# One transfer for the gate weights, and the first loads moved ahead of the opening barrier, in a fused attention and adapter kernel

## The chip, the cores and the metric

The kernel runs on one core of a Trainium2 chip. The metric is the device time of one execution in microseconds (us). The kernel before took 256.07 us (median of 3 runs, 255.68 to 256.32). Runs come with a state: "fast" unless they lie over 1.5% above the fastest of their kernel, "unknown" for a single run. The core has five instruction streams: TensorE (PE), VectorE (DVE), ScalarE (ACT), GpSimd (POOL) and SyncE (SP). Three of them issue transfers here: SyncE, ScalarE and GpSimd. The transfers are done by 16 DMA engines. Each load reports that it has landed by 16 increments of a semaphore. Below, a "ring" is the share of a load behind one of these increments, and a load has landed when the last of its 16 rings has.

## The reference, cut to what matters

```python
# q, k, v: 4 x 6400 x 256 float32
qn = q / (np.linalg.norm(q, axis=1, keepdims=True) + 1e-06)
kn = k / (np.linalg.norm(k, axis=1, keepdims=True) + 1e-06)
a  = softmax(kn.transpose(0, 2, 1) @ qn / tau)      # 256 x 256 per batch
x  = (v @ a).reshape(25600, 256)
logits = x @ w_gate                                  # 256 x 8; the two largest of 8 experts are kept
# delta = sum over the two experts of  weight * (x @ A[e]) @ B[e],   A[e]: 256 x 16, B[e]: 16 x 256
return x + delta
```

Only one thing of it matters: q and k of the first batch must be on the core before any matmul can run, and the gate weights, A and B (`moe_w_gate`, `moe_A`, `moe_B`) are small and needed much later, at about 35 us.

## The kernel before: the parts that matter

The first two columns of chunks of q and k come in as float32 by SyncE and ScalarE, whose transfers do not cast. ScalarE casts them. All else of q, k and v comes in through GpSimd, whose transfers cast to bf16 under way. The first such GpSimd load is the rest of the first piece of q (called "GpSimd's q" below), the second the same part of k ("GpSimd's k").

```python
    def load_consts():
        first = W["first"].rearrange("p c d -> p (c d)")
        W["A0"] = first[0:P // 4, 4 * C:8 * C].rearrange("p (e g r) -> p e g r", e=E, r=R)
        nc.sync.dma_start(W["A0"], moe_A.rearrange("e (p g) r -> p e g r", g=8))
        W["B0"] = first[:, 8 * C:9 * C]
        nc.scalar.dma_start(W["B0"], moe_B.rearrange("e r d -> (e r) d"))
        W["wg0"] = first[:, 9 * C:9 * C + CC * E].rearrange("p (cc e) -> p cc e", e=E)
        wg = moe_w_gate.rearrange("(p g cc) e -> g p cc e", g=4, cc=CC)
        for g in range(4):
            nc.scalar.dma_start(W["wg0"][g * (P // 4):(g + 1) * (P // 4)], wg[g])

    def do_load(s, what, b, i, c, n):
        # ... cut: choice of the tile t and the source src
            if (b, c) == (0, 0):
                # ... cut
                (nc.sync if what == "q" else nc.scalar).dma_start(W[what], src[b, :, 0:n, :])
                return
        nc.gpsimd.dma_start(t[:, c - c0:c - c0 + n, :], src[b, :, c:c + n, :])

    # ... cut; the steps are emitted in a planned order:
    for s in steps:
        do[s.key[0]](s, *s.key[1:])
        if s.key[0] == "load":
            n_load += 1
            if n_load == 2:
                load_consts()
            if n_load == 4:
                make_consts()
```

The program that is built from this has two blocks at its start. The first, called "main" below, is not in the kernel's text: GpSimd writes four constants (memsets), then every engine has a DRAIN instruction, then comes an opening barrier. The second block, the "body", holds the kernel.

## Time and profile before

| | before |
|---|---|
| time | 256.07 us |
| span in the profile | 254.4 us |
| PE busy | 85% |
| DMA engines | 90% busy or more in all but the first and last of 40 slices |
| first byte moves | 1.75 us |
| GpSimd's q issued, landed | 1.24 us, 10.22 us |
| GpSimd's k issued, landed | 1.90 us, 14.72 us |
| last matmul ends | 246.3 us |

First the strip of 40 equal slices and the DMA queues, from the page of the kernel before. A digit is a busy share in tenths, 9 being 90% or more. The queues show packets, megabytes and the share of the 16 engines' span that the packets took. q0 is GpSimd's, and here carries its casting loads. q1 and q10 carry what SyncE and ScalarE issue.

```profile
DMA  8999999999999999999999999999999999999994
...
q0 software_dynamic: 7488, 39.06, 74.7%
q1 hardware_dynamic: 3968, 26.61, 25.7%
q10 hardware_dynamic: 480, 0.40, 0.7%
```

Next, the timeline of the start of the kernel before: start, duration, engine, line, operation, and in brackets how long the engine was idle before and what released it ("issue": nothing that the profile shows).

```profile
0.34 0.10 POOL L926 MEMSET const-uint8-127<- 128x1 uint8 x1
0.74 0.40 ACTq L541 DMA_DIRECT2D y<-in_k_dram  x1
0.74 0.38 SPq L541 DMA_DIRECT2D y<-in_q_dram  x1
...
1.24 0.66 POOL L543 DMA_DIRECT2D qk<-in_q_dram  x1 [0.79 <-POOLq L926]
1.66 2.02 ACTq L483 DMA_DIRECT2D y<-in_moe_w_gate_dram  x4
1.90 0.54 POOL L543 DMA_DIRECT2D qk<-in_k_dram  x1
...
3.70 1.28 ACT L497 ACT_TABLE_LOAD   x1 [3.70 <-issue]
...
14.76 1.84 PEld L558 LDWEIGHTS <-qk 128*128 128x128 bf16 x10 [7.92 <-DMA qk<-in_k_dram]
```

SyncE and ScalarE issue their first loads at 0.74 us, right behind the barrier, and GpSimd at 1.24 us. ScalarE then spends 2.02 us on four gate transfers. From 14.76 us on PE works on what GpSimd's k brought. These waits are what the change aims at.

### The profile page before, as it was taken

To read this page: it belongs to the slowest core of one execution; us is meant where nothing else is said; L and a number is where in the kernel's file an instruction comes from. 1 tells how busy PE (TensorE), PEld (TensorE's weight loads), DVE (VectorE), ACT (ScalarE), POOL (GpSimd) and SP (SyncE) were. 2 spreads that over 40 slices of the span, in tenths; PEclk is the share of its full clock that TensorE was granted. 3 is DMA by queue.
4 is the path that set the end of the run, shared out by engine and by line. 5 is a ranking of instruction groups with operands and counts; after the bars stand their busy time and mean duration, and the time that the engine had idled before them with its cause. 6 is when DMAs were issued, how large, how long until landed. Compare 5 with 4: busy or idle time off the path is not lost.

```text
span 254.4 us, 6345 instructions
## 1 busy us (share of the span) xinstructions
PE 217.1 (85%) x2641; PEld 193.2 (76%) x2643; DVE 189.6 (75%) x483; ACT 166.7 (66%) x270; POOL 30.0 (12%) x58
## 2 busy tenths in 40 slices
PE   0165984899999998999989999889999979999970
PEld 0053962598999996799789998779999759999860
DVE  0055589779889977898979995689888878888910
ACT  3344446558786766888768667543777859768770
POOL 7000220040020002000130100510000200000000
PEclk9999997599999999999999999999999999999995
DMA  8999999999999999999999999999999999999994
GB/s 188 215 218 208 211 220 213 213 220 215 213 218 210 317 293 293 259 216 219 210 215 220 214 216 216 214 208 353 276 287 320 337 315 315 321 426 422 423 411 174
DMA packets 11964, 66.47 MB, mean 261 GB/s; under 512 B 1568, under 2 KB 2464, under 8 KB 7328
## 3 DMA queue, kind: packets, MB, share of 16 engines
q0 software_dynamic: 7488, 39.06, 74.7%
q1 hardware_dynamic: 3968, 26.61, 25.7%
q10 hardware_dynamic: 480, 0.40, 0.7%
q8 instruction: 20, 0.33, 0.5%
q14 instruction: 8, 0.07, 0.1%
HBM read 78.91 MB, written 26.21 MB: 413 GB/s over the span
## 4 chain that ended last, share of the span: by engine, by line
PE 54%; DMA 34%; DVE 3%; ACT 3%; POOL 2%; issue 1%; DVEq 0%; ACTq 0%; POOLq 0%
DMA qk<-in_k_dram 28%; PE Y_ps L877 13%; PE Y_ps L881 7%; PE T_ps L753 7%; DMA v<-in_v_dram 6%; PE ZL_ps L775 5%; PE gzT_ps L864 3%; PE acc_417 L558 2%; PE acc_418 L558 2%; PE acc_2620 L558 2%; PE acc_2621 L558 2%; PE Z_ps L844 2%; DVE a_bf L727 2%; POOL qk L543 1%; PE log_ps L790 1%
## 5 line engine op out<-in xcount | busy, mean ns | idle before, releaser
L586 DVE TENSOR_TENSOR ssq<-ssq,sq 128x1280 f32<-128x1280 f32 (+1 forms) x27 | 43.4, 1607 | 26.7 <-ACT sq L580 24.7
L877 PE MATMUL Y_ps<-a_bf,vT 128*128 128x256 bf16 x400 | 60.0, 273 | 0.0
L580 ACT ACTIVATE sq<-qk 128x1280 f32<-128x1280 bf16 (+1 forms) x27 | 36.8, 1364 | 25.9 <-DVE ssq L586 19.3
L733 ACT COPY y<-Y_ps 128x512 f32<-128x512 f32 x79 | 45.8, 587 | 12.2 <-PE Y_ps L881 9.6
L558 PEld LDWEIGHTS <-qk 128*128 128x128 bf16 x400 | 33.8, 103 | 24.9 <-DMA qk<-in_k_dram 15.3
L733 ACT COPY vT<-T_ps 128x1024 bf16<-128x1024 bf16 (+1 forms) x44 | 37.0, 871 | 7.7 <-PE T_ps L753 7.5
L877 PEld LDWEIGHTS <-vT 128*128 128x128 bf16 x400 | 37.6, 98 | 3.7
L881 PE MATMUL Y_ps<-ball,gzT 128*128 128x256 bf16 x200 | 38.2, 273 | 0.3 <-DVE gzT L735 0.3
L558 PE MATMUL acc_110<-qk 128*128 128x256 bf16 x50 | 15.0, 310 | 16.9 <-DMA qk<-in_k_dram 10.6
L753 PE MATMUL T_ps<-ident,v 128*128 128x128 bf16 x400 | 28.0, 224 | 0.6 <-DMA v<-in_v_dram 0.6
L543 POOL DMA_DIRECT2D v<-in_v_dram x20 | 12.2, 612 | 128.7 <-PE T_ps L753 81.5
L562 PEld LDWEIGHTS <-qk 128*128 128x128 bf16 x242 | 24.3, 100 | 3.4
L753 PEld LDWEIGHTS <-v 128*128 128x128 bf16 x400 | 24.6, 100 | 1.9 <-DMA v<-in_v_dram 1.5
L881 PEld LDWEIGHTS <-gzT 128*128 128x128 bf16 x200 | 19.4, 98 | 3.0 <-DVE gzT L735 0.6
L775 PE MATMUL ZL_ps<-waA_sb,vT 128*128 128x136 bf16 x280 | 19.6, 222 | 1.1 <-DVE waA_sb L721 0.9
L864 PE MATMUL gzT_ps<-ident,gz 128*128 128x128 bf16 x200 | 19.7, 219 | 0.3
L775 PEld LDWEIGHTS <-vT 128*128 128x128 bf16 x280 | 17.7, 98 | 1.8 <-issue 1.3
L735 DVE COPY gzT<-gzT_ps 128x512 bf16<-128x512 bf16 (+1 forms) x39 | 15.0, 390 | 5.5 <-PE gzT_ps L864 4.8
L580 ACT ACTIVATE ssq<-qk 128x1536 f32<-128x1536 bf16 x8 | 11.9, 1483 | 10.2 <-DMA qk<-in_q_dram 4.8
L735 DVE COPY y<-Y_ps 128x512 f32<-128x512 f32 x21 | 14.3, 690 | 3.3 <-PE Y_ps L881 3.3
L733 ACT COPY zl<-ZL_ps 128x272 f32<-128x272 f32 (+1 forms) x35 | 14.0, 447 | 3.1 <-PE ZL_ps L775 3.0
L567 PEld LDWEIGHTS <-qk 128*128 128x128 bf16 x168 | 14.8, 98 | 1.2 <-issue 0.2
(304 smaller groups left out, 440.9 us busy)
## 6 DMA issues: line engine op xcount, KB each, us to landing
out_dram<-y SPq DMA_DIRECT2D x18, 1280.0 KB, 17.8
v<-in_v_dram POOLq DMA_DIRECT2D x20, 640.0 KB, 20.3
qk<-in_q_dram POOLq DMA_DIRECT2D x7, 1088.0 KB, 24.0
qk<-in_k_dram POOLq DMA_DIRECT2D x7, 1088.0 KB, 28.9
qk<-in_q_dram POOLq DMA_DIRECT2D x2, 1024.0 KB, 18.5
qk<-in_k_dram POOLq DMA_DIRECT2D x2, 1024.0 KB, 22.8
out_dram<-y SPq DMA_DIRECT2D x4, 512.0 KB, 6.6
qk<-in_q_dram POOLq DMA_DIRECT2D x2, 512.0 KB, 17.4
```

What stands on the lines that cost most here:

```text
L558: nc.tensor.matmul(acc[ic][:, 0:256], kt[:, j, ic * P:(ic + 1) * P], qt[:, j, :], start=c == 0, stop=False, skip_group_check=True)
L562: nc.tensor.matmul(acc[ic][:, 256:384], kt[:, j, ic * P:(ic + 1) * P], kt[:, j, ic * P:(ic + 1) * P], start=False, stop=False, skip_group_ ...
L567: nc.tensor.matmul(acc[ic][:, 384:512], qt[:, j, ic * P:(ic + 1) * P], qt[:, j, ic * P:(ic + 1) * P], start=False, stop=c == NC - 1, skip_ ...
L580: nc.scalar.activation(out[:, 0:n, :], t[:, j:j + n, :], ACT.Square)
L586: nc.vector.tensor_tensor(out=t, in0=t, in1=held["sq", (w, b, g), ""][:, 0:n, :], op=OP.add)
L733: nc.scalar.copy(out, in_)
L735: nc.vector.tensor_copy(out, in_)
L753: nc.tensor.matmul(ps[:, ic, j, :], vt[:, c + j, ic * P:(ic + 1) * P], W["ident"], is_transpose=True, start=(ic + j == 0), stop=(ic == CC ...
L775: nc.tensor.matmul(ps[:, j, :], vT[:, ic, c + j, :], st[b]["waA"][:, ic, :], start=(j == 0 and ic == 0), stop=(j == n - 1 and ic == CC - 1 ...
L864: nc.tensor.matmul(ps[:, j, :], gz[:, j, :], W["ident"], is_transpose=True, start=(j == 0), stop=(j == n - 1))
L877: nc.tensor.matmul(ps[:, j, :], vT[:, ic, c + j, :], st[b]["a"][:, ic, :], start=(j == 0 and ic == 0), stop=False, skip_group_check=True)
L881: nc.tensor.matmul(ps[:, j, :], gzT[:, c + j - UNITS[u][0], :], W["B"], start=False, stop=(j == 1), skip_group_check=True)
```

## The change

Its intent: start the stream of transfers earlier, by issuing the first loads of SyncE, ScalarE and GpSimd before the opening barrier, and spare ScalarE three issues by fetching the gate weights in one transfer in place of four. The four parts of the gate weights are then spread over the partitions by four small DVE copies.

```diff
+def first_ahead(nc, names):
+    def move(nc):
+        main, body = nc.main_func.blocks[:2]
+        first = [i for i in body.instructions if i.name in names]
+        assert len(first) == len(names), (names, len(first))
+        rest = [i for i in body.instructions if i.name not in names]
+        at = next(n for n, i in enumerate(main.instructions) if type(i).__name__ == "InstMemset")
+        main.instructions = main.instructions[:at] + first + main.instructions[at:]
+        body.instructions = rest
+    nc.at_finalize(move)
 # ... cut: load_consts
-        wg = moe_w_gate.rearrange("(p g cc) e -> g p cc e", g=4, cc=CC)
-        for g in range(4):
-            nc.scalar.dma_start(W["wg0"][g * (P // 4):(g + 1) * (P // 4)], wg[g])
+        W["wg0"] = first[0:P // 4, 9 * C:9 * C + 4 * CC * E].rearrange("p (g cc e) -> p g cc e", g=4, e=E)
+        nc.scalar.dma_start(W["wg0"], moe_w_gate.rearrange("(p g cc) e -> p g cc e", g=4, cc=CC))
 # ... cut: do_wts
-        nc.vector.tensor_copy(W["wg"], W["wg0"])
+        for g in range(4):
+            nc.vector.tensor_copy(W["wg"][g * (P // 4):(g + 1) * (P // 4)], W["wg0"][:, g])
 # ... cut: do_load
-                (nc.sync if what == "q" else nc.scalar).dma_start(W[what], src[b, :, 0:n, :])
+                early.append((nc.sync if what == "q" else nc.scalar).dma_start(W[what], src[b, :, 0:n, :]))
                 return
-        nc.gpsimd.dma_start(t[:, c - c0:c - c0 + n, :], src[b, :, c:c + n, :])
+        load = nc.gpsimd.dma_start(t[:, c - c0:c - c0 + n, :], src[b, :, c:c + n, :])
+        if len(early) < 3:
+            early.append(load)
 # ... cut: behind the loop over the steps
+    first_ahead(nc, {i.ins.name for i in early})
```

So three loads, one of each issuing engine, now stand in "main" ahead of the memsets and the barrier.

More of the change, by code (lines that the diff above doesn't have):

```diff
@@ L479, in load_consts @@
         nc.scalar.dma_start(W["B0"], moe_B.rearrange("e r d -> (e r) d"))
-        W["wg0"] = first[:, 9 * C:9 * C + CC * E].rearrange("p (cc e) -> p cc e", e=E)
-        wg = moe_w_gate.rearrange("(p g cc) e -> g p cc e", g=4, cc=CC)
-        for g in range(4):
-            nc.scalar.dma_start(W["wg0"][g * (P // 4):(g + 1) * (P // 4)], wg[g])
+        W["wg0"] = first[0:P // 4, 9 * C:9 * C + 4 * CC * E].rearrange("p (g cc e) -> p g cc e", g=4, e=E)
+        nc.scalar.dma_start(W["wg0"], moe_w_gate.rearrange("(p g cc) e -> p g cc e", g=4, cc=CC))
     def make_consts():
@@ L901 @@
     n_load = 0
+    early = []
     for s in steps:
```

## The prediction

> **What bounds the kernel.** The 16 DMA engines. The strip of 40 slices has them 90% busy or more in every slice but the first and last, and HBM moves 413 GB/s over the 254.4 us span. PE is 85% busy. The chain of waits starts with 0.64 us before the first GpSimd issue, goes through k loads (28% of the span), v loads (5.5%) and PE work (54%). After PE's last matmul (246.3 us) the engines stay full until about 249 us, draining stores. Transfer work is fixed, so the end should move with the stream's start.
>
> **The start, before (timeline and windows of 0.25 us).** SyncE waits 0.7 us for the opening barrier; SyncE and ScalarE issue the first q, k at 0.74. GpSimd does four memsets (0.24 to 0.44), sits idle 0.79 us in the barrier, then issues q (1.24, 0.66 us) and k (1.90, 0.54 us). No byte moves before about 1.75 us. From 1.75 to 2.5 the engines move only 106 to 139 GB/s, from 2.5 on about 340. ScalarE spends 2.02 us (1.66 to 3.68) issuing four gate transfers of 2 KB, so its table load starts at 3.70 and the casts at 5.11.
>
> **What changes.**
> 1. First q, k issue: from 0.74 to about 0.05. First bytes at about 1.05 to 1.1 (same 1.0 us from issue to bytes): 0.7 us earlier.
> 2. GpSimd's q issue: from 1.24 to about 0.25, ending near 0.9. It pushes the memsets, and so the barrier, back by about 0.65 us: the other engines get through at about 1.4. GpSimd's k issue stays at about 1.9. No gap comes of that: the q load of 960 KB bf16 alone is over 4 us of transfer.
> 3. moe_A, moe_B go out 0.65 us later: harmless, needed at 34.5 us.
> 4. One gate transfer in place of four: three issues of about 0.49 us go (1.5 us of ScalarE), and 96 data packets and some semaphore packets of the 480 on that queue. That queue takes 0.7% of 16 engines' span, 1.8 us; I estimate 0.1 to 0.3 us of engine time back.
> 5. The table load starts near 2.4, casts at about 4.4, when q, k land. Worth little: PE then waits for k (14.76) anyway.
> 6. DVE: one copy of 0.17 us becomes four, at 36 us, off the chain.
>
> **On the path.** Items 1, 2 and 4: 0.7 us of earlier stream, up to 0.3 more because q's software queue joins about 1 us earlier and fills the weak stretch, and 0.1 to 0.3 from packets; sum 0.7 to 1.2. The engines are full throughout, so nothing later swallows it. The Trainium skill, "DMA: Bandwidth & Descriptors", section "Issuing engines are not separate DMA queues", says that all issuers run on the same 16 engines and that several issuers save only issue time; so I expect a shift, not more bandwidth.
>
> **Predicted: 255.1 us, 254.4 to 255.9.** Chances: faster by over 2% 0.01, within 2% 0.98, slower 0.01.
>
> **What the profile would show.** First bytes near 1.1 us; GpSimd's q issue before its memsets, k's still near 1.9; barrier release near 1.4; one gate issue; ACT table load near 2.4; first k load consumed near 14.0 instead of 14.76; PE busy unchanged; last matmul about 0.8 us earlier.
>
> **What would make it wrong.** The engines start later than the barrier wait suggests (gain under 0.4); the DMA engines are slow to ramp whatever is issued; the buffer waits of GpSimd's v loads (81.5 us for PE) swallow the shift; or the clock throttle falls differently in the stage near 50 us, where it granted 0.5 to 0.7.

## More of the kernel before

In the barrier the four other engines count up a semaphore with their drains. GpSimd drains, waits for the count of four, and releases the others.

Stretches of the start show how much is moved; the columns are the window, its length, the busy time of PE, PEld, DVE, ACT and POOL with counts, the granted clock, the mean busy share of the DMA engines, and GB/s. A share may exceed 1: a packet's whole duration is counted where the packet starts, and the durations overlap (over the whole span the shares of the five queues add up to 101.7%). So a share near 1 does not tell how much is moved.

```profile
0.00:3.00 3.00, 0.00 (x0) 0.00 (x0) 0.45 (x3) 0.00 (x0) 1.89 (x9) 1.00 0.40 79
3.00:8.00 5.00, 1.04 (x4) 0.44 (x4) 0.00 (x0) 2.51 (x4) 3.17 (x7) 1.00 1.10 258
8.00:14.00 6.00, 0.00 (x0) 0.00 (x0) 0.81 (x1) 2.85 (x2) 0.54 (x1) 1.00 1.07 219
...
212.00:246.00 34.00, 34.00 (x449) 31.56 (x448) 26.89 (x77) 26.34 (x49) 0.00 (x0) 1.00 1.01 389
```

The last line is of the end: PE is busy in all of its 34 us, and the DMA share is no higher than at 219 GB/s. The share alone does not show that the transfers bound the kernel there.

## The result, and the profile after

The changed kernel took 259.41 us (median of 5 runs: 257.03, 259.30, 259.41, 259.45, 259.83). The kernel before took 256.10 us in the same rounds. Ratios here and below are those worked out from the fast runs of both kernels. They are not quite the ratio of the medians quoted. This one is 1.0109, with a 95% interval of 1.0076 to 1.0141. The kernel became 1.1% slower, where the prediction had it 0.4% faster. The class "within 2%" held. The sign and the range (254.4 to 255.9) did not.

The profiled execution of the changed kernel is the fastest of the five, 257.03 us. First its strip and its smallest queue. The second digit of the strip has fallen from 9 to 6, and q10 has lost 144 packets.

```profile
DMA  8699999999999999999999999999999999999995
...
q10 hardware_dynamic: 336, 0.40, 0.5%
```

Then its timeline, with the lines that answer to those shown of before:

```profile
0.00 0.38 SPq L554 DMA_DIRECT2D y<-in_q_dram  x1
0.12 0.38 ACTq L554 DMA_DIRECT2D y<-in_k_dram  x1
0.73 0.66 POOL L556 DMA_DIRECT2D qk<-in_q_dram  x1 [0.73 <-issue]
...
1.49 0.12 POOL L943 MEMSET const-uint8-127<- 128x1 uint8 x1
8.88 0.37 ACTq L493 DMA_DIRECT2D y<-in_moe_B_dram  x1
...
9.27 0.47 ACTq L495 DMA_DIRECT2D y<-in_moe_w_gate_dram  x1
9.29 0.53 POOL L556 DMA_DIRECT2D qk<-in_k_dram  x1 [7.68 <-POOLq L943]
9.77 1.28 ACT L509 ACT_TABLE_LOAD   x1 [9.77 <-PEq L943]
...
16.92 0.13 PEld L573 LDWEIGHTS <-qk 128*128 128x128 bf16 x2 [4.03 <-DMA qk<-in_k_dram]
```

The first three loads do go out early. Then nothing is issued by any engine from 1.6 to 8.88 us. GpSimd's k goes out at 9.29 us in place of 1.90, and the weights that wait for it are loaded into PE at 16.92 us in place of 14.76. The stretches of this start, from the changed kernel, show the hole in the transfers:

```profile
4.00:6.00 2.00, 0.00 (x0) 0.00 (x0) 0.00 (x0) 0.00 (x0) 0.00 (x0) 1.00 1.07 219
6.00:7.50 1.50, 0.00 (x0) 0.00 (x0) 0.00 (x0) 0.00 (x0) 0.00 (x0) 1.00 0.91 189
7.50:8.00 0.50, 0.00 (x0) 0.00 (x0) 0.00 (x0) 0.00 (x0) 0.00 (x0) 1.00 0.11 15
8.00:9.50 1.50, 0.00 (x0) 0.00 (x0) 0.45 (x3) 0.00 (x0) 0.20 (x1) 1.00 0.00 0
9.50:10.00 0.50, 0.00 (x0) 0.00 (x0) 0.00 (x0) 0.23 (x1) 0.50 (x2) 1.00 0.12 30
```

The DMA engines are all but out of work from about 7.6 us, when most of GpSimd's q is in. The last packet ends at 8.23 us, and the next starts at 9.86.

What held the engines up is not among the counted instructions. The raw records of the trace hold the drains; start and duration in us:

```
            before              after
SP   DRAIN  0.000   0.007       0.431   0.127
DVE  DRAIN  0.116   0.010       0.108   0.010
ACT  DRAIN  0.137   0.008       0.539   0.141
PE   DRAIN  0.315   0.008       0.308   0.008
POOL DRAIN  0.309   0.188       0.806   7.829   (ends 8.635)
POOL releases the others   0.619         8.757
```

GpSimd's DRAIN takes 7.83 us in place of 0.19. It ends at 8.635 us, 0.085 us after the last of the 16 increments by which GpSimd's q reports that it has landed (8.55 us). SyncE and ScalarE drain in 0.13 and 0.14 us though their own loads land only at 2.92 and 3.55 us.

**Theory.** A GpSimd drain waits until the transfer that GpSimd itself has issued ahead of it has landed on all its rings. The barrier is then as late as that landing, every other issue stands behind the barrier, and the engines run dry between the end of q and the first byte of k.

**Rivals.** (R1) The drain waits for something else, such as GpSimd's descriptor work or the four memsets pushed behind the load. (R2) The loads of SyncE and ScalarE ahead of the barrier, or the gate transfer, cause the loss. A second question is why the earlier start that did happen earned nothing. The prediction counted on 0.7 to 1.2 us from it.

### The profile page after: what moved, and what is told of

Same layout as the page of the kernel before. It is cut to its first block, busy times and chain, and to the rows that moved or that the text cites. A ratio compares the mean times of both kernels' runs of the same rounds, so it can differ in the third digit from the quotient of the medians.

```text
span 255.7 us, 6344 instructions
## 1 busy us (share of the span) xinstructions
PE 215.6 (84%) x2643; PEld 192.1 (75%) x2643; DVE 189.9 (74%) x486; ACT 167.3 (65%) x270; POOL 30.0 (12%) x58
## 4 chain that ended last, share of the span: by engine, by line
DMA 59%; PE 28%; issue 3%; POOL 2%; DVE 2%; ACT 1%; POOLq 0%
DMA v<-in_v_dram 27%; DMA qk<-in_k_dram 21%; DMA qk<-in_q_dram 11%; PE Y_ps L892 9%; PE Y_ps L896 4%; PE T_ps L768 4%; PE gzT_ps L879 2%; PE ZL_ps L790 2%; PE acc_1620 L573 2%; PE acc_1621 L573 1%; PE Z_ps L859 1%; POOL qk L556 1%; PE log_ps L805 1%; PE acc_1621 L577 1%; PE acc_1620 L577 1%
## 5 line engine op out<-in xcount | busy, mean ns | idle before, releaser
L768 PE MATMUL T_ps<-ident,v 128*128 128x128 bf16 x400 | 27.0, 219 | 1.7 <-DMA v<-in_v_dram 0.9
L768 PEld LDWEIGHTS <-v 128*128 128x128 bf16 x400 | 23.6, 98 | 3.2 <-DMA v<-in_v_dram 2.8
L748 ACT COPY gzT<-gzT_ps 128x512 bf16<-128x512 bf16 (+1 forms) x21 | 10.3, 498 | 8.8 <-PE gzT_ps L879 8.5
```

The costliest lines, as they stand in the source:

```text
L748: nc.scalar.copy(out, in_)
L768: nc.tensor.matmul(ps[:, ic, j, :], vt[:, c + j, ic * P:(ic + 1) * P], W["ident"], is_transpose=True, start=(ic + j == 0), stop=(ic == CC ...
```

## The experiments

Fourteen experiments ran, three of them repeats of a kernel (y0, z1, z2), all with correct outputs. In the tables, k lands when the last of its 16 increments comes. Both this and the span are from the one profiled execution.

### Taking the change apart

**x1_no_pool**: the change, but GpSimd's load stays in its place.

```diff
         load = nc.gpsimd.dma_start(t[:, c - c0:c - c0 + n, :], src[b, :, c:c + n, :])
-        if len(early) < 3:
-            early.append(load)
```

> The whole change, but GpSimd's first load stays behind the barrier; SyncE's q and ScalarE's k go ahead of it. Theory D (GpSimd's drain in the opening barrier lasts until GpSimd's own transfer has landed; SyncE's and ScalarE's drains do not wait for theirs): GpSimd's drain about 0.2 us as in before, barrier open near 0.6 to 0.8 us, first bytes near 1.0 us, time about 255.4 us (255.0 to 255.8). Rival T (any transfer in flight holds the barrier or slows the fetch of instructions behind it): barrier open only after q, k land, near 3 to 3.6 us, time 257 to 259 us.

**x2_pool_only**: only GpSimd's load goes ahead; SyncE and ScalarE issue in their place.

```diff
-                early.append((nc.sync if what == "q" else nc.scalar).dma_start(W[what], src[b, :, 0:n, :]))
+                (nc.sync if what == "q" else nc.scalar).dma_start(W[what], src[b, :, 0:n, :])
-        if len(early) < 3:
+        if len(early) < 1:
```

> Only GpSimd's q load ahead of the barrier; SyncE and ScalarE issue q, k behind it; one gate transfer. Theory D: GpSimd's drain lasts until the 960 KB q load has landed (no other traffic beside it, so 6.5 to 7.5 us after its issue), barrier open near 7.5 to 8.2 us, time 257 to 260 us, worse than or like the full change, since q, k now also start behind the barrier. Rival T (SyncE's and ScalarE's transfers hold it): barrier near 1.4 us, time about 255.5 us.

**x3_gate_only**: only the gate transfer is changed.

```diff
-    first_ahead(nc, {i.ins.name for i in early})
```

> One gate transfer in place of four, nothing ahead of the barrier. Theory D: it is no part of the loss: 255.7 to 256.2 us, ScalarE's table load at about 2.2 us in place of 3.70. Rival G (the gate change itself costs, by its four DVE copies or by a 256-byte row transfer): slower than before by 0.5 us or more.

**x4_pool_after_drain**: all three loads ahead of the barrier, but GpSimd's stands right behind GpSimd's own drain.

```diff
-        main.instructions = main.instructions[:at] + first + main.instructions[at:]
+        pool = [i for i in first if str(i.engine).endswith("Pool")]
+        main.instructions = main.instructions[:at] + [i for i in first if i not in pool] + main.instructions[at:]
+        after = max(n for n, i in enumerate(main.instructions)
+                    if type(i).__name__ == "InstDrain" and str(i.engine).endswith("Pool"))
+        main.instructions = main.instructions[:after + 1] + pool + main.instructions[after + 1:]
```

> All three loads ahead as in the change, but GpSimd's q load stands just behind GpSimd's drain of the barrier (before it gathers the other engines). Theory D: the drain is about 0.2 us, the barrier opens near 0.8 to 1.4 us, q is issued near 0.6 us, time about 254.9 us (254.4 to 255.5), faster than before. Rival Q (GpSimd's queue itself is blocked by its first load for 7 us, wherever the load stands): k's issue near 9 us again, time 257 to 260 us.

| run | median us (range of fast runs) | ratio to before, 95% | GpSimd's drain | barrier opens | GpSimd's q, k issued | k lands |
|---|---|---|---|---|---|---|
| before | 256.03 in the same rounds | | 0.19 us | 0.62 | 1.24, 1.90 | 14.72 |
| changed | 259.41 (257.03 to 259.83) | 1.0109, 1.0076 to 1.0141 | 7.83 us | 8.76 | 0.73, 9.29 | 16.88 |
| x1_no_pool | 255.91 (255.33 to 256.05) | 0.9998, 0.9984 to 1.0011 | 0.19 us | 0.79 | 1.41, 2.07 | 14.30 |
| x2_pool_only | 258.86 (258.69 to 258.89) | 1.0110, 1.0094 to 1.0125 | 7.54 us | 8.48 | 0.73, 9.02 | not used |
| x3_gate_only | 255.85 (255.64 to 256.06) | 0.9994, 0.9981 to 1.0006 | as before | as before | 1.24, 1.90 | 14.73 |
| x4_pool_after_drain | 256.60 (256.29 to 256.93) | 1.0025, 1.0012 to 1.0037 | 0.19 us | 1.12 | 1.05, 1.71 | 16.23 |

The profiled execution of x2: 383.61 us at a mean granted clock of 0.58. Only its first 9 us are used, and the table has its three fast runs. Its timeline shows the same gap on GpSimd as the changed kernel's:

```profile
0.73 0.66 POOL L556 DMA_DIRECT2D qk<-in_q_dram  x1 [0.73 <-issue]
...
9.02 0.53 POOL L556 DMA_DIRECT2D qk<-in_k_dram  x1 [7.40 <-POOLq L943]
```

and x4's shows none, with the load only moved to the other side of the drain:

```profile
1.05 0.66 POOL L561 DMA_DIRECT2D qk<-in_q_dram  x1 [0.61 <-POOLq L948]
1.71 0.54 POOL L561 DMA_DIRECT2D qk<-in_k_dram  x1
```

What follows. The whole loss comes with GpSimd's load alone (x2), and it goes when that load is taken back (x1). R2 falls. In x4 the load is still ahead of the barrier and only behind the drain, and 2.8 us of the 3.3 are back. In that run and in x1 the memsets again run before GpSimd's load, so x1 and x4 alone do not rule out the memsets part of R1; the next experiment bears on that. x4 missed its expectation all the same: it was to be faster than before (254.4 to 255.5 us), and is slower, with an interval above 1. The rings of GpSimd's q land there from 9.26 to 11.55 us, and k at 16.23; more on this below. The gate part is harmless: x3 is 0.2 us faster by the medians, and its interval holds 1.

### A small load in front of the drain

If the drain waited for descriptor work or for memsets that come after a load, a tiny load would hold it as briefly as its own issue takes. If it waits for the landing, the drain shrinks to the time that a tiny load needs to land.

**xt_tiny**: x1 with a load of 16 elements by GpSimd ahead of the memsets, into a scratch tile.

```diff
     early = []
+    early.append(nc.gpsimd.dma_start(scrap, q_v[0, 0:1, 0, 0:16]))
```

> As x1_no_pool, with one more GpSimd transfer ahead of the barrier, of 16 elements on one partition, in place of the 960 KB load. Theory D (the drain lasts until the transfer has landed): the drain ends within 0.1 us after this transfer lands, at about 2.3 to 3 us, and the barrier opens right after, between the 0.8 us of x1_no_pool and the 8.77 us of the full change. Rival F (any GpSimd transfer ahead of a drain costs a fixed 7 to 8 us): barrier near 8.5 us whatever the size.

**y0_after_again**: the changed kernel once more, unaltered, as reference and for a second profile.

> The changed kernel unaltered, to see whether its two times (257.03 once, 259.3 to 259.8 four times) come back, and where they part. Theory D says that the drain ends with the q load in both, near 8.6 us; if the longer time comes of a later landing of q or of the first loads behind the barrier, the k load behind it lands later than 16.88 us by about 2 us in a long run; if it comes later in the kernel, k lands at 16.9 and the traces part after it. I expect 258 to 260 us as median.

From xt_tiny's timeline: GpSimd's issue of the tiny load takes 0.62 us, like the large one's 0.66, and the memsets stand behind it as in the changed kernel.

```profile
0.74 0.62 POOL L917 DMA_DIRECT2D scrap<-in_q_dram  x1 [0.74 <-issue]
...
4.65 0.55 POOL L556 DMA_DIRECT2D qk<-in_q_dram  x1 [3.07 <-POOLq L943]
```

| run | time, us | GpSimd's drain starts, lasts, ends | its own load lands | barrier opens |
|---|---|---|---|---|
| xt_tiny | 257.22 (one run) | 0.82, 3.16, 3.98 | 3.90 | 4.10 |
| x2_pool_only | 258.86 | 0.81, 7.54, 8.36 | 8.27 | 8.48 |
| changed | 257.03 (that run) | 0.81, 7.83, 8.64 | 8.55 | 8.76 |
| y0_after_again | 258.66 (that run) | 0.81, 9.43, 10.23 | 10.15 | 10.36 |

In four executions with four different landings the drain ends 0.08 to 0.09 us after GpSimd's load has landed. The memsets are the same in all four and the issue nearly so (0.62 to 0.66 us). That settles the theory against R1. The drain of xt_tiny was expected to end at 2.3 to 3 us, and ended at 3.98. The first q and k, ahead of its load by 0.7 us, were in transfer until 3.05 and 3.73 us, which may be why the load landed late; no run shows it.

The second profile also shows where two executions of the changed kernel part, which spreads from 257.0 to 259.9 us while the kernel before stays within 0.8 in any set of rounds. In y0's profile 15 of the 16 rings of GpSimd's q have landed at 8.21 us and the last one at 10.15 us. In the other profile they have landed at 8.25 and 8.55 us. The drain passes the slowest ring on to every engine: the span was 255.75 us in the one and 257.37 us in the other, 1.62 us apart for 1.60 us between the landings. Six more runs of the changed kernel took 257.48 to 259.86 us (median 259.40, ratio 1.0113, 1.0090 to 1.0137), so the first result holds. The runs of 259 us and over were not profiled. The granted clock is not what differs: it was 0.98 in the run of 257.03 us and in that of 259.41.

### Where the earlier start goes

With GpSimd's load out of the way, SyncE and ScalarE still issue 0.6 to 0.7 us earlier, and their q and k land about 1.8 and 1.1 us earlier (x1: 2.93 and 3.96 us, in place of 4.76 and 5.07). Yet x1 gains 0.1 us by the medians, and its interval holds 1. The next kernels try to collect the gain.

**x7_between**: SyncE's and ScalarE's first loads, and A, B and the gate weights, stand between their own engine's drain and its wait for the release, so that they cost the barrier nothing; GpSimd's q stands behind GpSimd's release.

**x12_qk_between**: the same for the first q and k only; all else as in x1.

```diff
-        main.instructions = main.instructions[:at] + first + main.instructions[at:]
+        def put(load, kind):
+            after = max(n for n, i in enumerate(main.instructions)
+                        if type(i).__name__ == kind and i.engine == load.engine)
+            while main.instructions[after + 1].name in names:
+                after += 1
+            main.instructions = main.instructions[:after + 1] + [load] + main.instructions[after + 1:]
+        for i in first:
+            put(i, "InstDrain")     # x7: "InstEventSemaphore" for GpSimd's
```

> All six first hardware-queue loads (q, k, moe_A, moe_B, gate) stand between their engine's drain and its wait for the release, and GpSimd's q load just behind the release, so no drain has a transfer ahead of it. Theory D: barrier opens near 0.65 us as in before. Theory C (x4_pool_after_drain lost because moe_A, moe_B and the gate were still queued when GpSimd's stream began, landing on some of the 16 rings as late as 13.4 us): here they are queued first and land on all rings by about 5 us, q's landings lie within 1 us of each other, k lands at 13.9 to 14.4 us in place of 14.72, time 255.2 to 255.8. If x4's loss comes of the early start of GpSimd's q alone: some rings lag again by 1 to 2 us and the time is 256.3 to 257.

> Only the first q and k of SyncE and ScalarE move: each stands between its engine's drain and its wait for the release, so neither drain waits and the barrier opens at 0.65 us as in before (0.82 in x1_no_pool); GpSimd's loads stay; one gate transfer. If an earlier first byte were passed on whole (the prediction's step): first bytes 0.65 us earlier, k landing at about 14.1 in place of 14.72, time 255.4 us. Theory L (hardware-queue transfers in flight when GpSimd's stream starts hold back some of the 16 rings, by a different amount in every run, and eat the gain): k lands between 14.1 and 15.7 us, time within 0.4 us of before.

**x8_late_consts**: x4, with A, B and the gate weights issued by ScalarE only after its two casts.

```diff
-            if n_load == 2:
-                load_consts()
+        if s.key[0] == "cast":
+            n_cast += 1
+            if n_cast == 2:
+                load_consts()
```

(In x8, A moves from SyncE's stream to ScalarE's as well.)

**x9_consts_pool**: x12, with A, B and the gate weights on GpSimd's queue behind its sixth load. **x9b_consts_pool_q_early**: x9, with GpSimd's q behind GpSimd's drain in main, as in x4.

```diff
-        nc.sync.dma_start(W["A0"], ...)      # A; B and the gate weights alike from nc.scalar
+        nc.gpsimd.dma_start(W["A0"], ...)
-            if n_load == 2:
+            if n_load == 8:
                 load_consts()
```

> x4_pool_after_drain with moe_A, moe_B and the gate issued by ScalarE behind its two casts, near 5 us, when GpSimd's stream is in full flow. Theory C: without them in the queue at the start no ring lags, q lands by 9.5 us on all rings and k by 14.2, time 255.2 to 255.8; they themselves land late (by 15 us), which nothing waits for before 34 us. If the lag comes of GpSimd's early q beside the first q, k: q's last ring at 11 us or later again, 256.3 to 257 us.

> x12_qk_between with moe_A, moe_B and the gate on GpSimd's queue behind its sixth load, so that no small hardware-queue transfer is left beside GpSimd's stream. Theory L1 (the small transfers are what holds back rings): q lands by 9.3 us, all rings within 1 us, k by 13.9, time 255.1 to 255.5 with little spread. Theory L2 (the first q, k of 256 KB themselves do it): rings still part by more than 1 us in some runs, time no better than 255.8 in the median.

> x9_consts_pool with GpSimd's q load moved up to just behind GpSimd's drain, so that it overlaps the first q, k most. Theory L1: no worse than x9_consts_pool, 254.9 to 255.4 us. Theory L2: rings part by 1 to 2 us at q's landing, time 256 us or more, as in x4_pool_after_drain and x8_late_consts.

| run | median us (range) | ratio to before, 95% | GpSimd's q issued | its rings land, first to last | k lands |
|---|---|---|---|---|---|
| before | 256.10, 255.91 | | 1.24 | 9.31 to 10.22 | 14.72 |
| x7_between | 256.28 (255.69 to 256.76) | 1.0000, 0.9987 to 1.0013 | 1.23 | 9.62 to 11.16 | 15.72 |
| x12_qk_between | 255.95 (255.58 to 256.38) | 1.0002, 0.9990 to 1.0015 | 1.24 | 9.34 to 11.18 | 15.74 |
| x8_late_consts | 256.94 (256.12 to 257.59) | 1.0029, 1.0013 to 1.0045 | 1.05 | 8.68 to 9.88 | 15.31 |
| x9_consts_pool | 257.09 (256.25 to 257.36) | 1.0037, 1.0020 to 1.0053 | 1.23 | 8.47 to 10.37 | 14.97 |
| x9b_consts_pool_q_early | 256.90 (256.14 to 258.02) | 1.0046, 1.0024 to 1.0068 | 1.06 | 8.47 to 9.71 | 14.27 |

No placement gains. My first explanation was that the many small packets of A, B and the gate weights hold some rings of GpSimd's load back. It falls: x8, x9 and x9b issue them only from 3.6 us (x8) or about 5 us on and are slower, not faster (x9 and x9b put three more loads on GpSimd's queue, so they are no clean test of that alone, but x7, with the small ones first, is no faster either).

The stretches of x12 show what happens in it instead. To be read against the same stretches of before, shown above:

```profile
0.00:3.00 3.00, 0.00 (x0) 0.00 (x0) 0.45 (x3) 1.36 (x2) 1.89 (x9) 1.00 0.59 173
3.00:8.00 5.00, 1.03 (x4) 0.43 (x4) 0.00 (x0) 1.25 (x3) 3.16 (x7) 1.00 1.08 192
8.00:14.00 6.00, 0.00 (x0) 0.00 (x0) 0.00 (x0) 2.73 (x2) 0.53 (x1) 1.00 1.03 210
```

Up to 3 us x12 moves 173 GB/s where before moved 79. From 3 to 8 us the engines are as busy as before (1.08 against 1.10) but move 192 GB/s in place of 258. Most of that difference is only a shift: SyncE's and ScalarE's loads, 0.55 MB of what before moves in this stretch, are half done by 3 us in x12 (0.28 MB left). The rest is loss. GpSimd's own packets fill more of the stretch in x12 (share 0.86 against 0.70) and move less (0.68 MB against 0.74). So over all 8 us x12 is no further, at 185 GB/s against 191. The first 16 packets of GpSimd's load took 586 or 587 ns each in before, without exception, and 1181 ns on average in x12 (up to 1836). Busy was not the same as moving.

**x13_q_delayed**: x12, with small memsets on GpSimd that delay its q until the loads of SyncE and ScalarE are through.

```diff
     early = []
+    for _ in range(26):
+        nc.gpsimd.memset(scrap, 0.0)
```

**z1_no_pool_again** and **z2_qk_between_again**: x1 and x12 unaltered, for second profiles.

> Run x12 with 26 small GpSimd memsets (one takes about 50 ns in the trace) ahead of GpSimd's q load: q and k still go ahead from SyncE and ScalarE (0.08 and 0.2 us), GpSimd's q issue moves from 1.24 to about 2.5 us, so that its first packets (1.4 us after issue in the run with GpSimd's load alone) start at about 3.9 us, when the hardware queues have moved all but a rest (their rate falls off after 3.9 us in x12). Theory L2 (the packets of the first hardware loads slow the first GpSimd packets and pull its 16 rings apart): mean packet time near 590 to 650 ns from the start instead of 1488 and 1007 ns, last ring of q 9.6 to 10.1 us instead of 11.18, k 14.2 to 14.6, time 255.3 to 255.8. Rival L3 (a GpSimd stream that starts early is slow in itself, whatever runs beside): mean of the first packets over 1000 ns, last ring of q after 10.6 us, time 256.2 or more. A third possibility, that it is chance: the repeat of x12 beside it shows other values than x12 did.

> Run x1 again, for a second profile. If the landing of GpSimd's q (9.75 us, rings 1.1 us apart) follows from the timing of the issues, it comes within 0.3 us of that again; if the parting of the rings is chance from execution to execution, it may land anywhere from 9.7 to 11.6 us, and the time follows it (about 0.75 us of time for each us of landing, as 255.33 went with 9.75 and 256.93 with 11.55).

> Run x12 again, for a second profile. If timing decides: GpSimd's q lands at 11.0 to 11.4 us again with first packets over 1000 ns. If chance: it lands anywhere from 9.7 to 11.6 us, and the first packets are as slow or not accordingly.

| run | time, us | GpSimd's q issued, first packet starts | its first 16 packets, mean (max) ns | rings land, first to last | k lands |
|---|---|---|---|---|---|
| before | 256.07 | 1.24, 4.35 | 586 (587) | 9.31 to 10.22 | 14.72 |
| x1_no_pool | 255.91 | 1.41, 3.67 | 707 (1164) | 8.62 to 9.75 | 14.30 |
| z1_no_pool_again | 256.08 (one run) | 1.41, 3.64 | 740 (1467) | 8.60 to 10.38 | 14.93 |
| x12_qk_between | 255.95 | 1.24, 3.75 | 1181 (1836) | 9.34 to 11.18 | 15.74 |
| z2_qk_between_again | 256.32 (one run) | 1.24, 3.75 | 1117 (1752) | 9.60 to 10.84 | 15.39 |
| x2_pool_only | 258.86 | 0.73, 2.10 | 1242 (1499) | 7.42 to 8.27 | not used |
| x13_q_delayed | 258.25 (257.75 to 258.34), ratio 1.0074, 1.0060 to 1.0087 | 4.78, 6.14 | 1270 (1707) | 11.60 to 12.34 | 16.90 |

The x13 experiment missed its own setting: the memsets took 157 ns each and not 50, and the delay became 3.5 us in place of 1.3, with the cost to match. From its timeline:

```profile
0.74 4.09 POOL L925 MEMSET scrap<- 1x16 bf16 x26 [0.29 <-POOLq L951]
...
4.78 0.66 POOL L563 DMA_DIRECT2D qk<-in_q_dram  x1
```

It still bears on the question, because GpSimd's q ran alone in it, as in x2; its time does not, since the issue was so late. In both, the last ring lands 7.54 to 7.56 us after the issue, and the first packet starts 1.36 or 1.37 us after it. The first 16 packets take 1242 and 1270 ns on average, the next 32 packets 597 and 604, and the rings land within 0.74 to 0.85 us of each other. So:

- Slow first packets come without any load beside them, when a stream of GpSimd's starts into idle engines (L3, right in this), here by 0.65 to 0.7 us over the steady 587 ns. In the kernel before they do not appear: its first packet starts 3.1 us after the issue, behind the other loads, and at full pace at once.
- When the stream starts among the loads of SyncE and ScalarE, the rings part: 1.1 to 1.9 us between the first and the last in x1, z1, x7, x8, x9, x9b, x12 and z2, and 2.29 us in x4, whose rings land from 9.26 to 11.55. Alone, it is 0.74 to 0.85. That agrees with L2 in this. But in the kernel before (0.91, with the stream at the tail of those loads) they hardly part, and in the changed kernel, whose stream starts among those loads too, they part by 0.87 us in one profile and 2.51 in the other. So overlap alone does not decide it. Which packets hold up which is not shown by any run.
- The repeats tell timing from chance. x12's slow first packets repeat, and its last ring is late again (11.18 and 10.84; 10.22 in before and 10.19 in x3, which starts alike), if outside the 11.0 to 11.4 expected. x1's does not keep its side of before (9.75 and 10.38): the gain of x1's first profile did not repeat. (The two pairs named in z1's expectation give 0.89 us of time for each us of landing, not 0.75.)

A load can be used only when its last ring has landed. The Trainium skill, "DMA: Bandwidth & Descriptors", section "Why a DMA increments its semaphore by 16 and not by 1", says that only the full 16 means that all data has landed, and the traces agree: each load reports in 16 increments, and ScalarE and PE start on q and k after the last (in before, 10.30 after 10.22 and 14.76 after 14.72 us). So a stream can be ahead by its bytes and behind by its landings, and z1 is the case: 0.11 MB ahead of before from 9 us on, and k lands 0.21 us later.

The end of the kernel takes part of what is left. The bytes of all packets, added up to a time (from the packets of the traces, in MB):

| up to | 3 us | 9 us | 20 us | 240 us | 252 us | span |
|---|---|---|---|---|---|---|
| before | 0.267 | 1.743 | 4.109 | 62.024 | 66.479 | 254.37 |
| z1_no_pool_again | 0.583 | 1.854 | 4.221 | 62.159 | 66.486 | 254.30 |
| x12_qk_between | 0.563 | 1.663 | 4.011 | 61.825 | 66.422 | 254.17 |
| changed | 0.557 | 1.557 | 3.650 | 61.099 | 66.045 | 255.75 |

In the last microseconds the engines run dry in the kernel before; in the changed one they are still full. The stretches of before, then those of the changed kernel:

```profile
248.00:250.00 2.00, 0.00 (x0) 0.00 (x0) 0.00 (x0) 0.00 (x0) 0.00 (x0) 0.81 0.88 355
250.00:252.00 2.00, 0.00 (x0) 0.00 (x0) 0.00 (x0) 0.00 (x0) 0.00 (x0) 0.50 0.46 182
```

```profile
248.00:250.00 2.00, 0.63 (x6) 0.31 (x4) 0.00 (x0) 1.17 (x2) 0.00 (x0) 1.00 1.02 410
250.00:252.00 2.00, 0.00 (x0) 0.00 (x0) 0.00 (x0) 0.00 (x0) 0.00 (x0) 1.00 0.94 375
```

So the tail evens out a lead or a lag of up to about half a microsecond: z1's lead of 0.135 MB at 240 us is 0.007 MB at 252 us, and x12's lag of 0.199 MB is 0.057, and neither span is longer than that of before. It also takes part of the changed kernel's lag. There k is 2.16 us late and the last matmul 2.34, so the delay comes through PE whole; but from the last matmul to the end it is 7.12 us in place of 8.08, and the span is 1.38 us longer.

## Why the prediction was wrong

- **"It pushes the memsets, and so the barrier, back by about 0.65 us: the other engines get through at about 1.4."** This is the step that failed. GpSimd's drain in the barrier waits for GpSimd's own load to land, and the others got through at 8.76 us in one profile and 10.36 in another. The prediction let the load delay the barrier by its issue alone (0.65 us), where what counted was its landing, 7.8 us after the issue began. In the kernel before, GpSimd's drain took 0.19 us, with no load ahead of it. The Trainium skill's "GPSIMD Engine Reference", section "2.1 Instruction dispatch", says of an instruction's completion that for writes the data has actually landed in SBUF. It says so of what GpSimd's own cores write, not of transfers or drains, so it does not settle the case. The runs do: 0.08 to 0.09 us from landing to the drain's end in four executions.
- **"GpSimd's k issue stays at about 1.9. No gap comes of that."** It follows from the step above and failed with it: k was issued at 9.29 us, and the engines were all but idle from about 7.6 to 9.9 us.
- **"GpSimd's q issue: from 1.24 to about 0.25."** Mis-sized: 0.73 us. GpSimd needed 0.73 us from the start here, and 0.6 us from the release to its issue in before.
- **"First q, k issue: from 0.74 to about 0.05. First bytes at about 1.05 to 1.1."** Right: issued at 0.00 and 0.12 us, first byte at 1.02 us.
- **"The engines are full throughout, so nothing later swallows it."** The second step that failed, on its own account, as x1, x7 and x12 show: the earlier start of SyncE's and ScalarE's loads remains, the barrier is fast, and the ratios are 0.9998, 1.0000 and 1.0002. They test the 0.7 us of earlier stream, not the earlier start of GpSimd's q (1.23 to 1.41 us in them); x4, with 1.05 us, is the nearest to that. A full busy share was read as a full stream, and it is not: in before it is 1.07 at 219 GB/s and 1.01 at 389. In x12 GpSimd's packets filled more time and moved less (0.68 MB in place of 0.74 from 3 to 8 us), and the last ring of its q came no earlier. In x1 and z1 the bytes are ahead (1.86 and 1.85 MB at 9 us in place of 1.74), the last ring of q is earlier once and later once, and the tail evens out what is left. Why no gain is left in x1's median is therefore not shown by one cause. The sentence cited from "DMA: Bandwidth & Descriptors", section "Issuing engines are not separate DMA queues", that several issuers save only issue time, does not decide this: it tells neither what an earlier start is worth nor of a loss of pace where streams overlap.
- **"moe_A, moe_B go out 0.65 us later: harmless."** Their issue went to 8.88 us in place of about 1.2, for the first reason above. No run shows harm from that in itself.
- **The gate transfer, "0.1 to 0.3 us of engine time back", and the table load.** q10 lost 144 packets and 0.2 points of its share (0.7% to 0.5%), and x3 was 0.2 us faster by medians, which is not told from zero. The table load comes at 2.15 us in x3 in place of 3.70, as reasoned, and is worth nothing, as predicted. In the changed kernel itself it came at 9.77 us, behind the barrier.
- **"PE busy unchanged."** Right: 217.1 us before, 215.6 after. "Last matmul about 0.8 us earlier" was wrong: 248.63 us in place of 246.29.

Of what the prediction named as able to make it wrong, the clock is not it: the kernel before took 256.28 us at a granted clock of 0.979 and again at 0.964 beside x1, and see above for the changed kernel.

What stays open: why GpSimd's stream starts at full pace in the kernel before, and how its rings come to part when it starts among other loads, by different amounts from run to run. Also open is a difference between time and span: 1.7 us in the kernel before, 1.8 in most runs, and 1.3 us in the four kernels or repeats where a load of GpSimd's stands ahead of its drain.

No version beat the kernel before. The intervals of x1, x3, x7 and x12 hold 1; x4, x8, x9, x9b and x13 are slower by 0.25 to 0.74%, x2 by 1.1%.

## What to carry to other kernels

Before moving an instruction across a barrier, look at each instruction of that barrier and ask what it waits for on its own engine: here a load that stood ahead of GpSimd's drain held back every engine until it had landed, while loads ahead of the drains of SyncE and ScalarE made the barrier 0.17 us later (0.79 in place of 0.62 in x1). A drain may not show among the counted work, so look for it in the raw records when all engines are idle at once and the release comes from one of them. And do not take an earlier start for an earlier finish: here loads that started 0.7 us earlier left the time where it was. Compare landings and GB/s, not the busy share.

## What the Trainium skill lacked or had wrong

- "GPSIMD Engine Reference", section "2.1 Instruction dispatch": completion is tied to data landed in SBUF, but the page does not say that a GpSimd drain waits for a transfer which GpSimd has issued. Nor does another page: "PSUM — Partial Sum Buffer", section "Engine vs sequencer instructions", has it that a drain waits until the engine is fully idle, and leaves open whether a transfer in flight counts. The runs show drains of 7.83, 9.43, 7.54 and (16 elements) 3.16 us, each ending 0.08 to 0.09 us after the landing; with no load ahead, 0.19 us.
- "Perfetto Trace Analysis", section "Sequencer-only Instruction (DRAIN, etc)": the profiled window of such an instruction is described as its execution, after its semaphore waits, with the sequencer and semaphores as the only actors. GpSimd's drain has a record of 7.83 us, which begins at 0.81 us and spans four memsets of the same engine (1.39 to 1.61 us) and the transfer.
- "VectorE: DVE Perf Modes", section "The DRAIN you can't avoid": drains of the runtime's own are given as about 12 ns on all five engines. The drains here belong to the opening barrier of the program, a kind for which the page has no figure. In the kernel before they take 7 to 10 ns on DVE, PE, SyncE and ScalarE and 188 ns on GpSimd; in the changed kernel SyncE's and ScalarE's take 127 and 141 ns behind a load.
- "DMA: Bandwidth & Descriptors", section "Latency and other measured facts": first byte about 0.6 us for loads of SyncE and ScalarE, about 1 us for GpSimd's, without a word from when it is counted. From the start of the issuing instruction the runs show 1.0 us to SyncE's first packet, and 1.36 to 1.37 us for GpSimd into idle engines, 1.98 in the changed kernel and 3.11 in the kernel before, behind other loads.
- The same page, section "Issuing engines are not separate DMA queues": it does not tell that a stream of GpSimd's which starts into idle engines has slow first packets (1242 and 1270 ns, then about 590 to 600), nor that its rings can part further when it starts among other loads (0.87 to 2.51 us between the first and the last, 0.74 to 0.85 alone).
